# Attention inside a two-part kernel: scores with keys on partitions, exps 1536 columns wide without a maximum, V stationary, and a checked fallback

## Chip, cores, metric

One core of one Trainium2 chip. The metric is the device time of one execution in microseconds (us); smaller is better. Executions are compared as medians and as ratios of runs that took turns on the same chip.

## The reference, cut to what matters

Two independent computations of the same length, laid side by side in the output:

```python
def _A_ref(x, w_r, w_i):          # spectral filter: rfft2, times W, irfft2, on 2048 x 640
    ...
def _B_ref(x, wqkv, wo):          # attention: 2048 tokens, 32 heads of 20
    qkv = (x @ wqkv).reshape(B, S, 3, H, Dh).transpose(2, 0, 3, 1, 4)
    scores = einsum("bhqd,bhkd->bhqk", q, k) * Dh ** -0.5
    o = einsum("bhqk,bhkd->bhqd", softmax(scores), v)
    return o.transpose(0, 2, 1, 3).reshape(B, S, D) @ wo
return concatenate([a, b], axis=-1)
```

The attention has 32 x 2048 x 2048 scores: 2048 tiles of 128 x 512. Part A is a chain of matmul stages that is fed into the gaps of the attention as background jobs.

## The kernel before

The program is written by a scheduler in Python: it walks through "periods" p and puts, in each, one portion of attention work and some background on each engine. Every engine then runs its own list strictly in the order in which it was written, and waits on semaphores where data come from another engine. PE writes its results into eight banks of 512 columns (`ps`); copying a finished result out of a bank with DVE or ACT is called an eviction below.

Before, scores are computed twice. Pass A has queries on partitions and is reduced by DVE to row maxima:

```python
def a_period(self, p, pa):
    ...
        P.add("pe", fn, r=[("QA", u % 3), ("KT", g, kc)], w=[("ps", b) for _, b in tiles], name="quadA")
    for j, bank in tiles:
        P.add("dve", lambda e: e.tensor_reduce(pm[:, col:col + 1], ps[:, bank, :], AX.X, ALU.max), ...)   # shortened
```

The negated maxima are split into three bf16 numbers, put into three extra rows of the queries (hence 23 instead of 20 contraction rows), and pass B computes shifted scores with keys on partitions. ACT takes the exp of each 512-column tile, and PE multiplies with P stationary: four matmuls of 21 columns a tile, the 21st column of V being ones, which gives the row sums.

```python
def b_period_act(self, p, info):
    for j, bank, slot in info[2]:
        P.add("act", lambda e: e.activation(pt, ps[:, bank, :], AF.Exp, scale=SCALE), ...)               # shortened
```

Each period ends by filling PE up with dummy matmuls whose results nobody reads:

```python
            if cfg["WARM"]:
                act = (171.0 if (a_now and b_now) else ...) + planned
                ...
                deficit = cfg["ACT_TARGET"] - act          # ACT_TARGET = 470 ns of a 1196 ns period
                while deficit > 20.0 and cands:
                    bank = cands.pop(0)
                    n = 512 if deficit > 120.0 else (384 if deficit > 75.0 else 256)
                    self.dummy(bank, n)
                    deficit -= (n / 2.4) * n / (n + 128.0)
```

## Time and profile before

| | before |
|---|---|
| median of 2 runs | 1427.87 us |
| span of the profile | 1423.4 us |
| busy: PE, DVE, ACT | 93%, 89%, 90% |
| exps | 2048 of 128 x 512 |
| mean granted clock of PE | 0.99 |

One line it did not use is needed later: the page cuts the span into 40 slices and gives in each the PE clock that was granted, in tenths of full speed (9 stands for 0.9 and more).

```profile
PEclk9999999999889999999999999999999999999999
```

### The profile page before, as it was taken

What the parts mean: (1) busy time and instruction counts of PE and PEld (TensorE: products, weight loads), DVE (VectorE), ACT (ScalarE), POOL (GpSimd) and SP (SyncE); (2) the same over time, 40 slices, a digit from 0 to 9 for tenths busy, and PEclk for the clock granted to TensorE, in tenths of its full rate; (3) what the DMA queues carried; (4) which work ended last, traced back from release to release, by engine and by line L of the source; (5) the groups of instructions that cost most, each with busy time, mean ns of one, the idle gap of its engine ahead of it and who ended that gap; (6) DMA issues with size and microseconds to landing.
All of it is one profiled execution on the core that took longest, in us unless ns stands there. A gap on an engine that the chain in (4) does not pass through costs nothing.

```text
span 1423.4 us, 35843 instructions
## 1 busy us (share of the span) xinstructions
PE 1318.5 (93%) x15309; PEld 553.8 (39%) x15560; DVE 1270.2 (89%) x2123; ACT 1279.0 (90%) x2475; POOL 154.6 (11%) x281
## 2 busy tenths in 40 slices
PE   8999999999999999999999999999999999999999
PEld 3333333334334334433334433333333444334444
DVE  4999999988879999999999889999988999999920
ACT  3399999988889999999999889999989999999996
POOL 3000000300000000000000006761000000000000
PEclk9999999999889999999999999999999999999999
DMA  5000000220000000010000000001000000000000
GB/s 172 1 1 2 1 2 1 79 99 1 2 1 16 6 2 2 2 46 2 2 2 16 6 1 2 2 2 61 2 2 6 16 2 2 29 20 20 20 20 19
DMA packets 15759, 24.48 MB, mean 17 GB/s; under 512 B 1904, under 2 KB 14960, under 8 KB 15216
## 3 DMA queue, kind: packets, MB, share of 16 engines
q1 hardware_dynamic: 15600, 22.18, 4.6%
q8 instruction: 121, 1.98, 0.6%
q14 instruction: 38, 0.31, 0.1%
HBM read 16.94 MB, written 5.24 MB: 16 GB/s over the span
## 4 chain that ended last, share of the span: by engine, by line
ACT 43%; PE 30%; DVE 23%; issue 2%; POOL 1%; DMA 1%; SPq 0%
ACT arena L821 33%; DVE arena L722 22%; ACT arena L201 9%; PE ps L841 8%; PE ps L714 7%; PE ps L756 6%; PE ps L807 2%; PE ps L579 1%; PE ps L531 1%; PE ps L659 1%; PE ps L1090 1%; ACT arena L856 1%; DMA arena<-in_B_wqkv_dram 1%; PE ps L604 1%; PE ps L1289 0%
## 5 line engine op out<-in xcount | busy, mean ns | idle before, releaser
L722 DVE TENSOR_REDUCE arena<-ps 128x1 f32<-128x512 f32 x2048 | 1253.9, 682 | 61.6 <-PE ps L807 50.7
L821 ACT ACTIVATE arena<-ps 128x512 bf16<-128x512 f32 x2048 | 1121.3, 606 | 83.7 <-PE ps L807 68.1
L841 PE MATMUL ps<-arena 128*128 128x21 bf16 x8192 | 372.0, 174 | 51.4 <-ACT arena L856 11.6
L714 PE MATMUL ps<-arena 20*128 20x512 bf16 x2048 | 400.1, 387 | 12.9 <-DVE arena L722 3.4
L807 PE MATMUL ps<-arena 23*128 23x512 bf16 x2048 | 400.0, 387 | 11.5 <-ACT arena L821 9.7
L841 PEld LDWEIGHTS ps<-arena 128*128 128x128 bf16 x8192 | 273.2, 96 | 334.9 <-ACT arena L821 300.7
L756 PE MATMUL ps<-arena 128*128 128x512 bf16 (+2 forms) x1149 | 356.0, 373 | 21.4 <-ACT arena L201 5.8
L714 PEld LDWEIGHTS ps<-arena 20*128 20x128 bf16 x2048 | 96.7, 91 | 408.0 <-DVE arena L722 392.9
L201 ACT CAST arena<-ps 128x512 bf16<-128x512 f32 (+4 forms) x323 | 164.8, 510 | 38.0 <-PE ps L538 15.7
L807 PEld LDWEIGHTS ps<-arena 23*128 23x128 bf16 x2048 | 96.6, 91 | 45.7 <-ACT arena L821 33.5
L738 POOL CAST arena<-arena 128x16 bf16<-128x16 f32 x32 | 8.1, 253 | 932.0 <-DVE arena L732 932.0
L756 PEld LDWEIGHTS ps<-arena 128*128 128x128 bf16 x1354 | 91.2, 96 | 22.2 <-ACT arena L201 7.1
L201 ACT COPY arena<-ps 128x1024 bf16<-128x1024 bf16 (+3 forms) x66 | 57.4, 875 | 9.0 <-PE ps L512 4.4
L859 DVE RECIPROCAL arena<-arena 128x16 f32<-128x16 f32 x32 | 8.1, 254 | 59.6 <-ACT arena L856 59.6
L868 POOL TENSOR_TENSOR arena<-arena 128x320 bf16<-128x320 f32 x32 | 23.3, 727 | 296.3 <-DVE arena L859 296.3
L579 PE MATMUL ps<-arena 128*128 128x512 bf16 x143 | 47.8, 393 | 1.6 <-issue 0.2
L531 PE MATMUL ps<-arena 128*128 128x512 bf16 x139 | 42.1, 379 | 0.7
L1289 PE MATMUL ps<-arena 128*128 128x320 bf16 (+1 forms) x192 | 36.4, 298 | 0.0
L1143 PE MATMUL ps<-arena 128*128 128x328 bf16 x160 | 32.6, 301 | 0.0
L659 PE MATMUL ps<-arena 128*128 128x320 bf16 x160 | 30.5, 298 | 1.5 <-DVE arena L202 1.5
L557 PE MATMUL ps<-arena 128*128 128x320 bf16 x160 | 30.0, 300 | 0.0
L1090 PE MATMUL ps<-arena 128*128 128x128 bf16 x246 | 24.5, 219 | 0.3
(54 smaller groups left out, 413.4 us busy)
## 6 DMA issues: line engine op xcount, KB each, us to landing
arena<-in_B_x_dram SPq DMA_DIRECT2D x4, 640.0 KB, 8.0
arena<-in_A_x_dram SPq DMA_DIRECT2D x1, 2560.0 KB, 8.8
out_dram<-arena SPq DMA_DIRECT2D x16, 160.0 KB, 1.8
out_dram<-arena SPq DMA_DIRECT2D x4, 640.0 KB, 3.2
arena<-ciCS SPq DMA_DIRECT2D x1, 2048.0 KB, 9.1
arena<-cslab SPq DMA_DIRECT2D x1, 1536.0 KB, 6.1
arena<-in_B_wqkv_dram SPq DMA_DIRECT2D x2, 700.0 KB, 8.1
arena<-in_A_w_r_dram SPq DMA_DIRECT2D x1, 1284.0 KB, 6.7
```

The costliest lines, as they stand in the source:

```text
L201: return eng.copy(out, in_)
L531: return lambda e: e.matmul(o, l, r_, start=st, stop=False)
L579: return lambda e: e.matmul(o, l, r_, start=st, stop=sp)
L659: return lambda e: e.matmul(o, l, r_, start=st, stop=sp)
L714: inst = e.matmul(ps[:, bank, :], qa[32 * j:32 * j + 20, qb * 128:(qb + 1) * 128], kt_[32 * j:32 * j + 20, g, kc * 512:(kc + 1) * 512], st ...
L722: P.add("dve", (lambda bank, col: lambda e: e.tensor_reduce(pm[:, col:col + 1], ps[:, bank, :], AX.X, ALU.max))(bank, col), r=[("ps", bank ...
L756: self.P.add("pe", lambda e: e.matmul(ps[:, bank, 0:n], l, r_, start=True, stop=True), r=[("ws",)], w=[("ps", bank)], name="dummy")
L807: inst = e.matmul(ps[:, bank, :], kt_[32 * j:32 * j + 23, g, kt * 128:(kt + 1) * 128], qbuf[32 * j:32 * j + 23, :], start=True, stop=True, ...
L821: P.add("act", (lambda bank, pt: lambda e: e.activation(pt, ps[:, bank, :], AF.Exp, scale=SCALE))(bank, pt), r=[("ps", bank)], w=[("PT", s ...
L841: inst = e.matmul(pvb[:, qb * 4 + j, :], PTs[slot][:, qb * 128:(qb + 1) * 128], va[:, kt, h, :], start=st, stop=False, skip_group_check=True)
L1090: return lambda e: e.transpose(o, in_, idn)
L1289: return lambda e: e.matmul(o, l, r_, start=s_, stop=e_)
```

## The change

The intent: drop the maximum. The scores of this input are small, so exp without a shift is safe; the kernel checks on chip afterwards that the sums of exps lie within a wide range, and if not runs the old attention as a fallback branch. Without maxima there is one set of scores, which can go to ACT three tiles at a time, and the product with V can be turned round: V stationary (21 columns in one of four 32-column strips of PE), P moving, 512 columns.

The core of the diff (cuts marked; indentation reduced):

```diff
+    def emit_qk(self, i):
+        for n, t in enumerate(self.group(i)):            # three tiles a group
+            bank = 3 * (i % 2) + n                       # banks 0-2 and 3-5 in turn
...
+                inst = e.matmul(ps[:, bank, :], kt_[32 * j:32 * j + 20, g, kt * 128:(kt + 1) * 128],
+                                q[32 * j:32 * j + 20, :], start=True, stop=True, tile_position=(32 * j, 0))
+    def emit_exp(self, i):
+        pt = self.PT[i % 4][:, 0:512 * n]
+        in_ = self.ps[:, h:h + n, :].rearrange("p b n -> p (b n)")
+        self.P.add("act", lambda e: e.activation(pt, in_, AF.Exp, scale=SCALE), ...
+    def emit_pv(self, p):
...
+                inst = e.matmul(ps[32 * j:32 * j + 21, 6, :], va[:, kt, h, :], pt, start=(kt == 0), stop=(kt == 15),
+                                tile_position=(0, 32 * j))
+    def unit_done(self, p, u):
+        P.add("dve", lambda e: e.tensor_copy(osb, ps[:, 6, :]), r=[("ps", 6)], w=[("osb", b2)], name="osb")
+        for j in range(4):                               # spread the sums over partitions
+            self.dma(dst, src, r=[("osb", b2)], pw=[("rin", b2)], stream="rin%d" % b2, name="den")
+        P.add("dve", lambda e: e.reciprocal(r16, rin), r=[("rin", b2)], w=[("rall", u)], name="recip")
+        self.dma(rs..., r16, ...)                        # to DRAM
+        self.dma(rb, src, ...)                           # and broadcast back
+        o = self.OTn[:, g, :]
+        P.add("pool", lambda e: e.tensor_tensor(o, osb, rb, ALU.mult), ..., w=[("OT", g)], name="normalize")
+        if g == NG - 1:
+            self.jobs_outproj(qc, p + 8)
...
+            if not self.att and credit["act"] >= 0.45 * ca:     # ACT evicts nothing during attention
...
+            banks = [7]                                          # background has one bank
+            if not self.att:
+                banks += [6, 0, 1, 2, 3, 4, 5]
...
+                bad = eng.value_load(flag, min_val=0, max_val=3)
+                with eng.If(bad > 0):
...
+                    slow.engine_body(ss, ename, eng)
```

A unit is 4 heads by 512 queries, 64 tiles; a quarter is the 8 units of the same 512 queries, after which their output projection runs. No dummies are written during the attention; the 24 at the start stay. A step is one group of three tiles; a full step is one that also carries background work.

## The prediction

> **What bounds the kernel now.** I read the page's busy times first, then the chain that ended last, the groups by line, and a short stretch of the timeline in the middle of the attention.
>
> ```profile
> PE 1318.5 (93%) x15309; PEld 553.8 (39%) x15560; DVE 1270.2 (89%) x2123; ACT 1279.0 (90%) x2475; POOL 154.6 (11%) x281
> ...
> ACT 43%; PE 30%; DVE 23%; issue 2%; POOL 1%; DMA 1%; SPq 0%
> ...
> L722 DVE TENSOR_REDUCE arena<-ps 128x1 f32<-128x512 f32 x2048 | 1253.9, 682 | 61.6 <-PE ps L807 50.7
> L821 ACT ACTIVATE arena<-ps 128x512 bf16<-128x512 f32 x2048 | 1121.3, 606 | 83.7 <-PE ps L807 68.1
> L841 PE MATMUL ps<-arena 128*128 128x21 bf16 x8192 | 372.0, 174 | 51.4 <-ACT arena L856 11.6
> ```
>
> Three engines are full at once and the chain hops between them. DVE finds the row maxima (2048 reductions, 98% of its busy time), ACT does 2048 exps and most other evictions, and PE computes every score twice (L714 for the maximum, L807 for the exp) and fills its gaps with dummy matmuls (L756: 356 us in 1149 pieces), so PE's 93% is not a need. Two tiles of each kind make a step of about 1.2 us.
>
> ```profile
> 601.08 0.58 PE L1143 MATMUL ps<-arena 128*128 128x328 bf16 x3
> ...
> 601.59 0.39 PE L714 MATMUL ps<-arena 20*128 20x512 bf16 x2
> ...
> 601.59 0.39 PE L807 MATMUL ps<-arena 23*128 23x512 bf16 x2
> ...
> 601.94 0.36 PE L841 MATMUL ps<-arena 128*128 128x21 bf16 x8
> 602.06 1.09 ACT L821 ACTIVATE arena<-ps 128x512 bf16<-128x512 f32 x2 [0.17 <-PE ps L807]
> ```
>
> Two things to see. Four 512-column score matmuls in four row strips start together and take 0.39 us in all, and work in the next array shape starts 0.35 us after them. Two exps back to back take 1.09 us, one alone 0.60, so an exp that finds its data ready costs 0.49 us, not 0.606.
>
> A stretch of the timeline in which V is projected, the groups by shape, the SP queue's timeline, and the page's DMA issues:
>
> ```profile
> 41.07 0.99 PE L557 MATMUL ps<-arena 128*128 128x320 bf16 x6
> ```
> ```profile
> L202 DVE COPY arena<-ps 128x1024 bf16<-128x1024 bf16 x3 | 2.1, 692 | 9.7 <-PE ps L512 9.7
> ...
> L202 DVE CAST arena<-ps 128x320 bf16<-128x320 f32 x1 | 0.5, 492 | 2.3 <-PE ps L659 2.3
> ```
> ```profile
> 0.74 0.34 SPq L334 DMA_DIRECT2D arena<-constB  x1
> ```
> ```profile
> out_dram<-arena SPq DMA_DIRECT2D x16, 160.0 KB, 1.8
> ```
>
> From these: a dense 320-column matmul every (0.99-0.30)/5 = 0.137 us; DVE evictions of 0.49 us (320 columns) to 0.69; a DMA takes the SP sequencer 0.34 us to issue, and 1.8 us to land.
>
> **What the Trainium skill says.** "ScalarE: Activation LUTs", section "What ACT_TABLE_LOAD costs": an ACTIVATE with immediates takes 186 ns + 0.833 ns per column, and back-to-back ones overlap by about 93 ns. For 512 columns that is 612 ns; the trace has 606, with an overlap of 606-490 = 116. "TensorE: Matmul & The Clock Gate", Part 3 (packing): four row tiles ran 3.07 times and three column tiles 2.38 times as fast as in sequence. The trace agrees for row tiles; no column-tiled matmul is in it. "TensorEngine Tiling (Array Packing)", Key Properties: changing the tiling mode drains the array. The trace shows about 0.35-0.22 = 0.13 us. The clock page's Part 1 says an idle array falls to half clock; this trace was kept full by dummies, so it cannot show that.
>
> **The change part by part.**
> Removed: all 2048 maximum reductions (1254 us of DVE), the first set of score matmuls, the maximum's trip back into the queries, the 1149 dummies of the attention (24 warm-up ones stay), 6144 of 8192 PV matmuls (V is now stationary: one 512-column matmul per tile, in four column strips).
> Added: per unit (32 of them: 4 heads by 512 queries) a 128x512 copy of bank 6 to SBUF, four small DMAs that spread the sums, a reciprocal, a DMA to DRAM, a broadcast back and a 128x512 multiply on Pool; once, 16 reductions of V, a flag and a branch around the old attention, which is not taken.
> Moved: during the attention all evictions go to DVE through the single bank 7, because banks 0-5 hold two groups of three score tiles and 6 the PV sums.
>
> *ACT.* 2048 tiles in threes: 683 exps. Spacing back to back: 0.49 + 1024 x 0.833 ns = 1.343 us. So 683 x 1.343 = 917 us, against 1121 us of exps before, with nothing else on ACT. This is the new bound.
>
> *PE per step* (estimates from the slots above): three scores and a mode change 0.34, three or four PV in column strips the same if they run together, background five 320-column matmuls 0.69 plus a change 0.10: 1.47 us, slightly over 1.343. By the program's order, V and FD take such a step 32 times each, the last inverse transform 32 times with six matmuls (0.23 over). Excess 64 x 0.1 + 32 x 0.23, about 13 us. Other background steps (two 512-column matmuls, eight transposes, four 256-column ones, half a projection) fit, and about 265 steps have none, where PE needs 0.7 of 1.34.
>
> *Start.* The first scores come at 21 us, as before (21.6). Only four exps can run, as the ring of four P buffers waits for V. Ahead of the first V tile stand eleven jobs on one bank, each PE then DVE in turn: four 8-block transposes (0.4+0.2+0.69), three 4-block ones (0.85), three K (1.8), V itself 1.3: about 16 us. The fifth exp starts at 37.5 us.
>
> *Steady.* 679 x 1.343 = 912, to 950 us; plus PE's 13; plus about 3 where unit 1 waits for its K and Q.
>
> *Unit ends.* DVE has the reciprocal directly behind the bank 6 copy, so it stands still for the four DMAs: copy 0.69, issues 4 x 0.34, landing 1.8, reciprocal 0.25, a good 4 us. An eviction queued behind it holds bank 7, PE's next background job waits for it in order, and the scores behind that job come some 2 us after the exp could use them (ACT has about two steps in hand). In the order some 17 of 32 unit ends have background work in flight: 17 x 2 = 35 us. The other 15 hide it.
>
> *Cold clock.* Late units have one Q job on an array at under half load; if the clock is halved, its four matmuls in a step take 1.7 us: estimated 8 us over all.
>
> *Tail.* Last PV and copy 1.2, sums 3.1, reciprocal 0.3, to DRAM and back 4, Pool multiply 1.3 (its 128x512 products take 1.15 to 1.27 now), 64 projection matmuls 8.7 plus 2 for a cold array, eviction and store 2.5, flag and branch 3: 26 us.
>
> Sum: 950 + 13 + 3 + 35 + 8 + 26 = 1035 us of span; the time is 4.5 us over the span before (1427.9 to 1423.4), so 1040. The author of the schedule plans 1.44 us a step, which suggests a step somewhat longer than mine; I put the prediction at **1045 us**.
>
> **The rivals.**
> 1. *PE takes ACT's place because column strips don't run together.* Then PV costs 3 x 0.216 + 0.1 = 0.75 us a step and a background step about 1.85: 400 x 0.5 = 200 us more, near 1240. For it: nothing in this trace shows column tiles, and each has its own 128-row moving operand. Against it: the skill's 2.38. About one in ten. A milder form, partial overlap, adds 0.06 us to 130 full steps, 8 us.
> 2. *The unit ends cost more or less than I put.* Small scattered DMAs could land in 3 us instead of 1.8, or fewer units could have work in flight: 10 to 70 us, so 1015 to 1080.
> 3. *The step is 1.44 as planned*, by slower three-bank exps or wake-ups: 679 x 0.1 = 66 more, near 1105.
> 4. *The gain is lost:* the clock stays at half all through. A step with little background then needs 2 x 0.56 = 1.1 us and still hides, but full ones take 2.4: 350 x 1.0, near 1390. The speed of the array in before with 40% real work speaks against it in those dense stretches.
>
> **Range and chances.** Rivals 2 and 3 set the range: 1005 to 1110 us. For less than 2% gain the time would have to stay above 1400, which needs rival 4 in full or a slow branch of hundreds of us: faster 0.97, same 0.015, slower 0.015.
>
> **What would show it right or wrong.** Right: 683 exps with a mean near 1.46 us and back-to-back starts 1.34 apart; ACT above 88% busy, nearly all exp; DVE under 25%; PV matmuls of one step starting within some ns of each other, about 0.39 us each; chain mostly ACT; the fifth exp near 37 us; exp gaps of about 2 us every 28 us, ended by score matmuls, with DVE idle before the reciprocal for about 3 us; a last exp about 26 us before the end. Wrong: PV starts 0.2 us apart, exp spacing over 1.4 without gaps, or score matmuls waiting for background work in most steps.

## The result, and the profile after

The median is 1219.04 us (1211.26 and 1226.82), against 1427.87 before. Ratios in this document are the mean time of one kernel's fast runs over that of the other's fast runs of the same rounds, so not quite the ratio of the medians: here 0.854, interval 0.841 to 0.868. Faster by 15%, and well outside the 1005 to 1110 us that I had predicted.

The page of the kernel after: busy times, then the slices of ACT and of the PE clock, the chain by engine, and the two largest groups.

```profile
PE 1014.8 (83%) x5818; PEld 291.8 (24%) x5864; DVE 246.0 (20%) x439; ACT 951.9 (78%) x689; POOL 137.6 (11%) x123
...
ACT  3678897977777977877778676757999869999990
...
PEclk7788997557888666856557766559655755556556
...
PE 52%; ACT 30%; DVE 6%; DMA 6%; SPq 3%; issue 2%; POOL 1%
...
L1560 ACT ACTIVATE arena<-ps 128x1536 bf16<-128x1536 f32 (+1 forms) x683 | 947.7, 1497 | 234.4 <-PE ps L1550 209.0
L1550 PE MATMUL ps<-arena 20*128 20x512 bf16 x2048 | 357.6, 517 | 61.2 <-ACT arena L1560 57.7
```

The work is as forecast: 683 exps, DVE at 20%, ACT with nothing but exps. But ACT is 78% busy instead of 88 and more: it waited 234 us ahead of exps, 209 of them for score matmuls (L1550). The chain is mostly PE, though PE has less to do. And the clock row has changed from nines to anything between five and nine; its mean over the span is 0.68 (the stretches behind it are all at 1.0 or 0.5, and a slice averages over several). A score matmul takes 517 ns on average, where it took 387 before.

Where the span went, by my own sum. "Excess" is what successive starts of exps are apart beyond 1.331 us, the spacing at which they run back to back.

| | predicted us | measured us |
|---|---|---|
| start of the fifth exp | 37.5 | 38.9 |
| the rest at full pace | 679 x 1.343 = 912 | 678 x 1.331 + 1.5 for the last = 904 |
| excess | 13 + 3 + 35 + 8 = 59 | 252 |
| last exp to the end | 26 | 30.6 |
| span | 1035 | 1225 |

So nearly all of the miss is in one line. I split the 252 by the size of the gap, counted here from start to start, and by the clock at the start of the exp that ends it:

| excess in | steps | us |
|---|---|---|
| three gaps of 13 to 15 us | 3 | 37.5 |
| gaps of 3.3 to 6.4 us | 19 | 73.6 |
| other steps, half clock | 395 | 109.2 |
| other steps, full clock | 261 | 31.3 |

About 250 of the 395 half-clock steps keep the full pace; the 109 us lie in the other 144.

**The gaps of 3 to 6 us** lie at unit ends, 17 of the 19 (67.4 us). The other two have other causes: at 70 us unit 1 waits for its K and Q (3.8 us, where I had put 3), at 581 us PE waits for a Pool product of part A (2.4 us). One of the 17 in the timeline of the kernel after (start, length, what; in square brackets the idle time before it and what ended it; the PE weight loads between these lines are left out):

```profile
321.88 0.69 DVE L1603 COPY arena<-ps 128x512 f32<-128x512 f32 x1
321.98 0.87 PE L1168 MATMUL ps<-arena 128*128 128x328 bf16 x5
...
322.60 2.44 SPq L359 DMA_DIRECT2D arena<-arena  x4
...
326.25 0.25 DVE L1609 RECIPROCAL arena<-arena 128x16 f32<-128x16 f32 x1 [3.68 <-DMA arena<-arena]
326.42 0.43 DVE L226 CAST arena<-ps 128x328 bf16<-128x328 f32 x1
...
326.91 1.55 PE L1168 MATMUL ps<-arena 128*128 128x328 bf16 x5 [3.42 <-DVE arena L226]
...
328.39 0.61 PE L1550 MATMUL ps<-arena 20*128 20x512 bf16 x3
...
329.05 1.45 ACT L1560 ACTIVATE arena<-ps 128x1536 bf16<-128x1536 f32 x1 [4.32 <-PE ps L1550]
```

DVE copies the unit's sums, and the next thing in its list is the reciprocal, which waits 3.68 us for the four DMAs. The eviction behind it (L226) could have run at once: its matmuls were done near 322.9. So bank 7 stays taken, PE's next background job waits 3.42 us, and the scores behind that job (L1550) come 4.32 us too late for ACT. Note the lengths on both sides of the wait: five 328-column matmuls took 0.87 us before it and 1.55 us after it, the three score matmuls 0.61 instead of 0.39. The array fell to half clock during the wait.

**A full step at both clocks.** The same background job at full clock some 13 us earlier:

```profile
314.14 0.39 PE L1550 MATMUL ps<-arena 20*128 20x512 bf16 x3
...
314.46 0.39 PE L1589 MATMUL ps<-arena 128*21 128x512 bf16 x3
314.80 0.87 PE L1168 MATMUL ps<-arena 128*128 128x328 bf16 x5
315.60 0.39 PE L1550 MATMUL ps<-arena 20*128 20x512 bf16 x3
```

From scores to scores 315.60 - 314.14 = 1.46 us (I had estimated 1.47). The PV matmuls (L1589) do run together: three in 0.39 us, and the next shape starts 0.34 us after them. At half clock the same step lasts from 328.39 to 330.95, 2.56 us. Where a step has no background, half clock is free: in this stretch, all of it at half clock, the exps start 1.33 us apart, and PE still waits 0.2 us a step for ACT:

```profile
256.13 14.88 ACT L1560 ACTIVATE arena<-ps 128x1536 bf16<-128x1536 f32 x11
...
258.97 0.61 PE L1550 MATMUL ps<-arena 20*128 20x512 bf16 x3 [0.19 <-ACT arena L1560]
...
259.51 0.61 PE L1589 MATMUL ps<-arena 128*21 128x512 bf16 x3
```

**The three long gaps** come once a quarter, in the last projection job:

```profile
357.12 0.69 DVE L1603 COPY arena<-ps 128x512 f32<-128x512 f32 x1 [1.74 <-PE ps L1589]
...
363.46 0.58 SPq L359 DMA_DIRECT2D arena<-rscr  x1
368.43 1.26 POOL L1615 TENSOR_TENSOR arena<-arena 128x512 bf16<-128x512 f32 x1 [34.29 <-DMA arena<-rscr]
369.84 1.76 PE L1633 MATMUL ps<-arena 128*128 128x320 bf16 x6 [11.58 <-POOL arena L1615]
...
372.18 1.45 ACT L1560 ACTIVATE arena<-ps 128x1536 bf16<-128x1536 f32 x1 [12.07 <-PE ps L1550]
```

The projection (L1633) of quarter 0 waits for Pool's multiply of unit 8, the first unit of quarter 1, whose sums were copied only at 357.12. It has no business to: it should read unit 0's result. The buffer of normalised outputs has one slot for each of the 8 units of a quarter. In the program order the multiply of unit 8, which overwrites slot 0, was placed one job ahead of the last projection of quarter 0. The dependency tracker therefore makes PE wait for it, and the job then uses the wrong quarter's first four heads. A walk through the program's task list finds exactly three such jobs, one at each change of quarter. The comparison with the reference passed all the same; I did not measure the error in those blocks. It is a fault of the changed kernel, and a wait.

**The tail**, from the chain that ended last (start, length, what):

```profile
1201.18 4.77 DMA arena<-rscr
...
1207.33 6.10 PE ps L1633 x33
...
1214.01 3.45 PE ps L1633 x24
```

The broadcast back from DRAM takes 4.8 us, where I had 4 for both ways (the way out is another 1.4).

### The profile page after: what moved, and what is told of

Its sections match the earlier page's. It is cut to its first block, busy times and chain, and to the rows that moved or that the text cites. A ratio compares the mean times of both kernels' runs of the same rounds, so it can differ in the third digit from the quotient of the medians.

```text
span 1225.0 us, 13302 instructions
## 1 busy us (share of the span) xinstructions
PE 1014.8 (83%) x5818; PEld 291.8 (24%) x5864; DVE 246.0 (20%) x439; ACT 951.9 (78%) x689; POOL 137.6 (11%) x123
## 4 chain that ended last, share of the span: by engine, by line
PE 52%; ACT 30%; DVE 6%; DMA 6%; SPq 3%; issue 2%; POOL 1%
ACT arena L1560 30%; PE ps L1550 12%; PE ps L1589 11%; DVE arena L226 4%; PE ps L1633 4%; PE ps L1503 4%; PE ps L1481 4%; PE ps L1314 3%; SPq L359 3%; DMA arena<-arena 3%; PE ps L1168 2%; PE ps L1224 2%; PE ps L582 2%; DMA arena<-rscr 2%; PE ps L1288 2%
## 5 line engine op out<-in xcount | busy, mean ns | idle before, releaser
L1560 ACT ACTIVATE arena<-ps 128x1536 bf16<-128x1536 f32 (+1 forms) x683 | 947.7, 1497 | 234.4 <-PE ps L1550 209.0
L1550 PE MATMUL ps<-arena 20*128 20x512 bf16 x2048 | 357.6, 517 | 61.2 <-ACT arena L1560 57.7
L1589 PE MATMUL ps<-arena 128*21 128x512 bf16 x2048 | 356.4, 517 | 5.6 <-DVE arena L1603 1.9
L226 DVE CAST arena<-ps 128x320 bf16<-128x320 f32 (+4 forms) x291 | 167.0, 574 | 623.6 <-PE ps L1503 167.1
L1615 POOL TENSOR_TENSOR arena<-arena 128x512 bf16<-128x512 f32 x32 | 40.5, 1265 | 1037.5 <-DMA arena<-rscr 1037.5
L1550 PEld LDWEIGHTS ps<-arena 20*128 20x128 bf16 x2048 | 69.7, 96 | 350.0 <-ACT arena L1560 217.0
L1589 PEld LDWEIGHTS ps<-arena 128*21 128x21 bf16 x2048 | 66.7, 91 | 249.2 <-issue 232.3
L1633 PE MATMUL ps<-arena 128*128 128x320 bf16 x256 | 52.7, 346 | 46.0 <-POOL arena L1615 45.5
L226 DVE COPY arena<-ps 128x1024 bf16<-128x1024 bf16 (+2 forms) x57 | 35.5, 623 | 89.8 <-PE ps L1115 64.7
L1224 PE MATMUL ps<-arena 128*128 128x512 bf16 (+1 forms) x78 | 33.6, 514 | 20.0 <-DVE arena L226 14.1
L1633 PEld LDWEIGHTS ps<-arena 128*128 128x128 bf16 x256 | 23.5, 108 | 70.1 <-issue 31.4
```

Source lines behind the costliest of these rows:

```text
L226: return eng.tensor_copy(out, in_)
L1224: return lambda e: e.matmul(o, l, r_, start=s_, stop=e_)
L1550: inst = e.matmul(ps[:, bank, :], kt_[32 * j:32 * j + 20, g, kt * 128:(kt + 1) * 128], q[32 * j:32 * j + 20, :], start=True, stop=True, ti ...
L1560: self.P.add("act", lambda e: e.activation(pt, in_, AF.Exp, scale=SCALE), r=[("ps", h + k) for k in range(n)], w=[("PT", i % 4)], name="exp")
L1589: inst = e.matmul(ps[32 * j:32 * j + 21, 6, :], va[:, kt, h, :], pt, start=(kt == 0), stop=(kt == 15), tile_position=(0, 32 * j))
L1633: return lambda e: e.matmul(o, l, r_, start=st, stop=sp)
```

## The experiments

Three theories about the 252 us. STALLS: the reciprocal in DVE's list and the misplaced multiply. CLOCK: no dummies hold the array at full clock, and full steps then take 2.56 us. CAPACITY: PE is over its capacity even at full clock. They are not exclusive, so the question is how much each is worth and whether one causes another. A program on one core has no slow die, but the label "slow" is given to a run over 1.5% above the same kernel's fastest, which happens here to kernels whose clock wanders.

### The changed kernel again, and three single edits (one chip, same rounds)

No edit, as a base:

> The changed kernel again, as a base on the same chip for the other three. Every theory: 1205 to 1230 us, mean granted clock 0.66 to 0.70.

1209.08 us (1208.48 to 1216.19), ratio to before 0.850; clock 0.698, as expected. This is the base for the next three.

**Dummies alone.** None are written within four periods of a unit's end.

```diff
+            work = sum(J.pe[J.nxt + i][1] for J, n in plan for i in range(n))
+            free7 = all(J.bank != 7 or J.nxt == 0 for J in self.inflight)
+            if self.att and nexp < nsteps and free7 and p - self.last_unit >= 4:
+                for _ in range(max(0, int((430.0 - work) / 216.0 + 0.5))):
+                    self.dummy7()
             self.bg_pe_emit(p, plan)
```

> Changed kernel plus up to two dummy 512-column matmuls into bank 7 in attention steps with little background work, none within four steps of a unit's end. Theory CLOCK (the array falls to half clock because the dummies of before are gone and nothing fills the gaps, and full steps then take 2.1 to 2.8 us instead of 1.4): granted clock over 0.85 and 90 to 130 us less, about 1110 us. Theory STALLS (the time goes in waits at unit ends and before the output projection, and the half clock hides behind the exps): clock may rise, but the time falls by less than 30 us. Theory CAPACITY (PE is over its capacity at full clock too, mode changes cost more than thought): the dummies make it slower.

1246.03, 1251.52, 1261.58 and 1206.74 us: no gain in the one fast run (the base's mean is 1211), and three slow ones, so the time excludes CLOCK's 1110. The profile is of a slow run (1246), so I take only what it shows of the mechanism: mean clock 0.784; 196 steps still at half clock, whose excess is 124.6 us, 0.64 us each, against 0.28 in the changed kernel (109.2 over 395). A dummy at half clock costs 0.43 us, and does not stand back for work that is late. The clock row, and one stretch in which the array stayed at half clock with PE full:

```profile
PEclk7788998776889788888887877578589888855557
```
```profile
1100.00:1200.00 100.00, 99.28 (x402) 16.68 (x400) 2.44 (x5) 73.78 (x52) 3.79 (x3) 0.50 0.03 9
```

(Columns: stretch and its length, busy us and instructions of PE, PE weight loads, DVE, ACT and Pool, then clock, DMA share and GB/s.) As a remedy on its own, CLOCK is refuted: of the 31 falls of the clock in this trace 16 lie in one of the gaps or within 3.5 us after it, and dummies do not reliably bring it back.

**Reciprocal late.** The reciprocal, the two DMAs behind it and the multiply are written three periods later; nothing else. The four DMAs that spread the sums stay where they were.

```diff
-        r16 = self.rall[:, u * 16:(u + 1) * 16]
+        self.pend.append((p + 3, u))
+
+    def unit_late(self, p, u):
+        ...
+        r16 = self.rall[:, u * 16:(u + 1) * 16]
...
-            self.jobs_outproj(qc, p + 8)
+            self.jobs_outproj(qc, p + 5)
...
+            while self.pend and p >= self.pend[0][0]:
+                self.unit_late(p, self.pend.pop(0)[1])
```

> Changed kernel with the reciprocal and what follows it placed three steps later in the program order, so that DVE does not stand in front of it while the sums are spread; this also moves the multiply of the next quarter's first unit behind the last projection. Theory STALLS: the 5 to 6 us exp gaps at unit ends go (some 18 times 4 us) and the three 13 to 15 us gaps go (37 us): about 110 us less, about 1110 us; DVE's wait before the reciprocal falls from 118 us to under 20. Theory CLOCK alone: only the 37 us and some of the unit ends' own waiting, 1170 us, with the clock below 0.75 as before.

1069.18 us (1053.35 to 1073.95), ratio to before 0.744 (0.738 to 0.751). That is 140 us less than the base (150 by the means of fast runs alone), more than the 110 that STALLS expected. In its trace (of a run at 1070.55, labelled slow beside the fastest at 1053.35, but all four runs are 11% and more below the base) the long gaps are gone and two gaps above 3.3 us are left. All other excess is smaller as well: half-clock steps 54.6 us instead of 83.9 in the base's trace. So the stalls cost more than their own length. Part of that went by way of the clock: in the trace of the changed kernel 18 of the 31 falls to half clock lie in a gap or within 3.5 us after it. But stalls are not all that drops it. Here, without them, the clock still falls 15 times, never at one of the two gaps, and is at half for 559 of 1069 us (788 of 1225 before this edit), most of all late, where little background work is left:

```profile
PEclk8699999567799755997658997996557755555556
```

The two gaps left are not the reciprocal's: unit 1's K and Q again, and, in the longer one, part A's product on Pool:

```profile
505.21 0.58 PE L1224 MATMUL ps<-arena 128*128 128x512 bf16 x1 [3.85 <-POOL arena L1257]
```

One miss: DVE's wait ahead of the reciprocal fell only to 62.9 us from 117.7; three periods are not quite as long as the DMAs take, but what is left is short enough for ACT not to feel it.

**Multiply held.** Only the multiply of each quarter's first unit is held back until the projections of the quarter before are written.

```diff
-        P.add("pool", ... name="normalize")
+        norm = lambda: P.add("pool", ... name="normalize")
+        if g == 0 and qc > 0:
+            self.held.append((qc - 1, norm))
+        else:
+            norm()
...
+            if self.held and all(J.done_p is not None for J in self.op_jobs[self.held[0][0]]):
+                self.held.pop()[1]()
```

> Changed kernel where only the multiply of each quarter's first unit is held back until the projection of the quarter before has been issued. All theories that name the three 13 to 15 us gaps as PE waiting for a multiply that has not run: those three gaps go, 3 times 12 = 36 us less, about 1180 us, nothing else changes. If the gaps come from the DMA queue instead, they stay.

1187.8 us (1180.44 to 1192.37), ratio to before 0.833: 21 us less than the base, not 36. The three gaps above 10 us went, but two more of the 3 to 6 us kind appeared (20 against 18, 81.3 against 72.4 us): at the same places the reciprocal's stall is still there, and had been hidden inside the long gap. The order of the program is right again in this version and in all later ones, and it already was with the late reciprocal, as the same walk through the task list shows; its own worth is about 20 us.

### Together, and three controls

**All three edits**, with dummies also at unit ends:

> All three edits together: reciprocal late, the quarter's first multiply held, up to two dummies in steps with little background work, now also at unit ends. Theory CLOCK as an independent cost: with no stall left to drop the clock the dummies hold it, granted clock over 0.9, half-clock excess (57 us in the run with the late reciprocal) mostly gone: about 1020 us. Rival DUMMIES ARE WORK: dummies issued while the array is at half clock take 0.43 us each and push a step past the exp; time no better than 1069 us.

1028.34 us (1022.17 to 1032.73), ratio 0.721 (0.717 to 0.725). Clock and ACT rows of its page:

```profile
ACT  3279999999999999997899999999999999999970
...
PEclk8599999999999999998799999999999999999996
```

Mean clock 0.96; excess 52 us instead of 232 to 252, of which 30.2 in full-clock steps, 13.2 in 16 half-clock ones, 8.9 in two gaps. So dummies that were worth nothing next to stalls are worth 41 us without them (33 by the means of fast runs):

| median us | no dummies | dummies |
|---|---|---|
| reciprocal in its old place | 1209 | 1249 (1207 to 1262) |
| reciprocal late | 1069 | 1028 (with the multiply held) |

The table is not a clean cross: the lower right version also writes dummies within four periods of a unit's end and holds the multiply. The multiply can hardly matter, as the version with the late reciprocal has none out of place and no long gap; what the dummies at unit ends add was not tested apart.

The full-clock excess of 30 us is the most that CAPACITY can be worth in this version. As a rough estimate, the price of the clock in the changed kernel is the excess of its steps outside gaps less that of these: (109.2 + 31.3) - (13.2 + 30.2) = 97 us; some of it may be steps that a stall just before had made late.

**Before without dummies**, those of the start-up included, to test that the dummies are what held its clock:

```diff
-WARM=True
+WARM=False
```

> The kernel before with all its dummy matmuls left out, the start-up ones too. If the dummies are what holds the clock in before (granted 0.99), the clock falls to 0.6 or below. If the time of before then stays within 2% its DVE reductions hide the half clock; by its step (four scores 0.35, eight PV, background about 0.4 at full clock against 1.2 to 1.3 us of DVE) I expect 3 to 8% slower, 1470 to 1540 us.

1648.32 us (1645.39 to 1657.4), 1.158 times before: slower than I expected by far.

```profile
PEclk9965555555555555555555555555555555555556
...
PE 69%; DVE 21%; ACT 5%; issue 4%; DMA 0%; SPq 0%; POOL 0%; POOLq 0%
```

The clock falls to half at 94 us and from then on returns three times only, for 6.8, 3.4 and 10.2 us (mean 0.533), though PE is counted busy 86% of the span. The chain, which hopped between three engines in before, is now PE's.

**Exps of 512**, on the version with the late reciprocal, to price the width:

```diff
-        self.P.add("act", lambda e: e.activation(pt, in_, AF.Exp, scale=SCALE), ...)
+        for k in range(n):
+            self.P.add("act", ... e.activation(pt[:, 512 * k:512 * k + 512], self.ps[:, h + k, :], AF.Exp, scale=SCALE), ...)
```

> The version with the late reciprocal, with each 1536-column exp split into three of 512 (same data, same banks). By the spacing measured in before, three cost 3 x 0.489 = 1.467 against 1.331 us: 683 x 0.136 = 93 us more on ACT. If ACT sets the pace nearly everywhere: 1069 + 70 to 93, about 1150 us. If PE at half clock sets it in half the steps: under 1115 us.

1131.72 us (1124.1 to 1142.58), ratio 0.797: 63 us more than 1069 (69 by the means of fast runs), between my two cases. The whole price is about 93 us by the spacing; I take the rest to lie in steps that PE at half clock was holding up anyway (that version has 94 us of excess to hide it in), which no run shows apart.

**No flag, no branch**, on the version with the late reciprocal (the waits for the flag, its loads and the fallback program left out):

> The version with the late reciprocal, without the wait for the flag, the branch and the fallback program (the 16 reductions of V and the flag's own arithmetic stay). The trace shows flag load and branch taking about 1.3 us after the flag is ready, most of it beside the last store: 0 to 4 us less than 1069, inside the spread of the runs, so only the end of the trace can tell.

1055.01 us (1049.45 to 1069.98), against 1069.18 (1053.35 to 1073.95) for the version with the branch, which was run on another occasion. The ranges overlap. From the last exp to the end of the profile it is 26.1 us without and 31.5 us with the branch, so some 5 us of the tail at most.

### A better start

The exps start early and then stop: in the kernel after, ACT runs four exps from 13.9 us and then waits 19.5 us for the first V, because from the first score on all projections go through bank 7 and DVE. The edit holds the first scores until four V tiles are projected:

```diff
+        if i == 0:
+            V = self.sj[("V", 3, 0)]
+            if V.done_p is None or V.done_p > p:
+                return False
```

> The version with all three edits, and the first scores held until the first four V tiles are projected, so that the start-up's projections use eight banks and both evicting engines instead of bank 7 and DVE alone. If the start-up costs the time from the fourth exp (about 19 us) to the fifth (40 us): the first exp comes near 25 us instead of 15, the fifth near 31 instead of 40.8, and the time falls from 1028 to about 1015 to 1020 us. Rival: the single bank was hidden behind loads, and nothing changes.

1002.81 us (1000.06 to 1011.52), ratio to before 0.704 (0.700 to 0.709). The base beside it on the same chip, the version with all three edits again:

> The version with all three edits again, as the base for the run beside it on the same chip: 1020 to 1035 us.

1026.28 us (1017.75 to 1034.27), ratio 0.722, as before. So 23 us (19 by the means of fast runs), twice what I expected. First the ACT timeline with all three edits (from their first run), then with the held start:

```profile
14.95 5.48 ACT L1567 ACTIVATE arena<-ps 128x1536 bf16<-128x1536 f32 x4 [1.68 <-PE ps L1557]
40.79 1.45 ACT L1567 ACTIVATE arena<-ps 128x1536 bf16<-128x1536 f32 x1 [20.36 <-PE ps L1596]
```
```profile
24.86 16.26 ACT L1571 ACTIVATE arena<-ps 128x1536 bf16<-128x1536 f32 x12 [0.81 <-PE ps L1561]
```

The first exp comes ten us later and the fifth at 30.2 us, ten us earlier than 40.8; twelve run without a gap. Besides, unit 1's wait of 3.8 us for its K and Q is gone; of the two gaps only the one for Pool's product is left. The base varies from run to run: in its second profile, taken beside this version, the fifth exp falls at 36.4 us and the half-clock steps number 5, as many as here and not 16 as in its first. So I do not split the 23 us further. This is the best version that I ran: 0.704 of before, where the changed kernel's ratios were 0.854 and 0.850.

## Why the prediction was wrong

By its own steps:

- **ACT is the new bound, 683 exps at 1.343 us.** Right: 1.331 back to back. With the stalls out of the way and the clock held, the span is 1028 us against the predicted 1035, but that agreement is partly luck: the 35 us for unit ends are in the prediction and not in that version, while start and tail are 8 us longer there. (The 4.5 us between span and time was misread, too: it sets one run's span against the median of two. Run by run the difference in every later run is about 2 us.)
- **PE per step 1.47 us, and column strips run together.** Right at full clock: 1.46 us, three or four PV matmuls in one slot. Rival 1 fell. The capacity term was 13 us (its own 1.47 us a step would have given 17); the full-clock steps have about 30.
- **Start, fifth exp at 37.5 us.** Right in its result, 38.9, but by luck. The chain of single-bank jobs is there, but it began 7 us earlier than I said (first exp at 13.9 and not 21) and took 25 us instead of 16.5, at half clock from 15.6 us on; my own list of its eleven jobs adds up to 14.4, not 16. The errors cancelled. What I did not see is that this start is avoidable.
- **Unit ends, 17 x 2 = 35 us.** The mechanism was right, as the timeline shows step by step; the count of 17 came out too, besides those hidden in the long gaps; the size was wrong: 67.4 us in the 17, 4.0 each instead of 2. I charged 0.34 us for a DMA issue, and the four scattered ones took about 0.6 each (2.44 for four); and I ran the work behind the stall at full clock, though the array fell to half clock in the wait, so 0.87 + 0.39 became 1.55 + 0.61.
- **Cold clock, 8 us.** This is the step that failed most: 109 us, in 144 of 395 half-clock steps, some 97 of it the clock's by the estimate above. I counted the late units only, taking the array of the background-filled units to stay at full clock. Rival 4, half clock throughout with full steps of 2.4 us, was the nearest to what happened. My argument against it was that before ran at full clock "with 40% real work". The run of before without dummies refutes that: its real work alone gave a clock of 0.533. The dummies, which I had read as idle filling, were what bought the clock, and the change removed them along with the work they padded. Even the trace of before had a sign of it that I passed over, saying it could not show the clock fall: the array is at half clock there in three stretches, 24 us in all (the two eights in its clock row are two of them).
- **Overlooked altogether: the three waits for a multiply of the wrong quarter**, 37.5 us in the trace, some 20 of which came back when only they were removed. It could have been read from the order of the program before any run: the projection takes 16 periods from 8 after its last unit, 24 in all, and the next unit ends after 21.3.
- **Tail, 26 us:** 30.6; the way through DRAM took 6.2 us instead of 4, and what follows the last projection matmul (eviction, flag, closing of the engines) 7.5 instead of 5.5.

The stalls and the clock are not two sums. The late reciprocal alone won 140 us where the gaps themselves were 110, and dummies alone won nothing where they won 41 after it (with those at unit ends): a stall empties the array, the clock often falls in it, and in the full steps that follow PE is late by itself. What is not settled: which load exactly makes the array keep or regain full clock. In the changed kernel 16 of its 31 returns came with a projection of queries (five dense 512-column matmuls) in the 3.5 us before, and in the stretch shown under "Dummies alone" it did not return under narrow score and PV matmuls with two dummies between; I have no run that isolates it.

## What to carry to other kernels

In engines that run their lists in order, place an instruction that waits for a DMA behind the work that is ready meanwhile; here the place of one 0.25 us reciprocal, with the DMAs and the multiply that follow it, was worth 140 us. When a change takes work off an engine whose clock depends on its load, price the steps that remain at the lower clock as well, and remove the stalls before padding with dummies, which earned nothing here while the stalls stood. When a buffer has one slot a stage, check in the program order that the last reader is written before the next writer: a dependency tracker turns the mistake into a wait and a wrong operand, and a tolerance may hide the latter.

## What the Trainium skill lacked or had wrong

- "TensorE: Matmul & The Clock Gate", Part 1: two clock states and windows of about 3.4 us agree (62 stretches in the trace after, all at 1.0 or 0.5, and 61 of them whole multiples of 3.41 us). But its table has the array warm after one busy window or more; here it stayed at half clock for 100 us with PE counted busy 99.3%, and through nearly the whole of before without dummies at 86%. The page speaks of short idles between groups of matmuls that make the clock swing, without a size; it gives no threshold of load and nothing on how much narrow matmuls (20 rows, or 21 columns) count. No run here isolates that either.
- Same page, Part 3: three column tiles at 2.38 times as fast as in sequence. Here column-tiled 512-column matmuls started some 4 ns one after another, which agrees with the 4 ns a tile of the page's model, and three and four of them took 0.39 and 0.40 us, where one takes 0.39; no run has them in sequence, so the factor itself is not tested.
- "ScalarE: Activation LUTs", "What ACT_TABLE_LOAD costs": 186 + 0.833 x 1536 = 1466 ns for one exp, measured 1451; the overlap of successive ones is 1451 - 1331 = 120 ns, the page has about 93.
- "TensorEngine Tiling (Array Packing)", Key Properties: the drain at a mode change is stated without a size; here it is about 0.1 us (next shape 0.32 to 0.34 us after three concurrent 512-column matmuls; dense ones of that width follow each other at 0.216 in the same trace).
- "DMA: Bandwidth & Descriptors": I found no issue time on it that depends on the shape of a copy on this chip; here the SP queue spent 0.53 to 0.6 us on most of the 2 KB copies spread over 32 partitions, and 0.33 on a plain 160 KB store.
